# Attention with routing: one operand of routing's VectorE operations in PSUM, low parts of weights behind the row normalisation

## The chip, the cores and the metric

The kernel runs on one core of a Trainium2 chip. The metric is the device time of one execution in microseconds (us). Each engine has its own instruction stream: TensorE (PE in the rows) multiplies and transposes into PSUM, VectorE (DVE) and ScalarE (ACT) work on SBUF and PSUM, GpSimd (POOL) works on SBUF here, and SyncE (SP) issues DMAs. Engines wait for each other by semaphores.

## The reference

Four sequences of 768 positions with 8 heads of 64 go through attention with 4 sinks and a window of 128. The 3072 resulting rows of 512 then go through a mixture of experts in two levels: a group of four and an expert of four inside it, 16 experts with a hidden width of 1024.

```python
keep = is_sink | in_window                  # rel >= 0 and rel < 128
scores = np.where(keep, scale * q @ k.T, -1e9)
a = softmax(scores); x = (a @ v) as [N, D]  # N 3072, D 512
g_idx = argmax(x @ w_group); g_w = softmax(x @ w_group)[g_idx]
for g in range(G):
    xg = x[g_idx == g]
    e_idx = argmax(xg @ w_expert[g]); e_w = softmax(...)[e_idx]
    for e in range(Eg):
        out[tokens of g, e] = g_w * e_w * (relu(xg @ w1[g, e]) @ w2[g, e])
```

## The kernel before

All instructions of one engine run in the order in which the code is written (class `Pinned`; nearly all of them show its line 105, so the rows go by the names of tiles). Attention is a loop over 24 query tiles of 128 rows (line 1225), software-pipelined: iteration i scores tile i, and finishes tiles i-1 (`a`) and i-2 (`b`). Per iteration TensorE does, in order: scores of the first four heads into PSUM tile `ps0`, values of the second half of tile `b` (`po`), scores of the other four heads into `ps1`, transposes of the weights (`tp`), the transposed rows of `b`, the router logits (`ps<-wsd,xT`, in spare columns 208 to 247 of `ps0`), values of the first half of `a`, and sums over the sinks.

VectorE does `maxima` for both halves (COPY_PREDICATED and four reductions each, out of `ps0` and `ps1` into `sm` and `st`), the logits' normalisation `lw`, the rows' normalisation `xt` out of `po`, and two kinds of extra work. `po` has one buffer, so the values of the next iteration wait for `xt`. ScalarE does the exponentials and evacuations; GpSimd masks the window's weights (`halves`: `pw<-pw,tri`, 128x512, with both inputs in SBUF, twice per iteration).

The first kind of extra work on VectorE is routing. The 24 tiles are routed in four batches of six (`route_batch`, line 362). Three of them run while attention does: batch 0 alone, batch 1 with the pick of the first expert to load (`pick_id`, line 524), batch 2 with the second; the fourth runs after attention. A batch is a generator; `unit(k)` and `routing` take one step of it, one or two small VectorE instructions, at fixed places of an iteration: between the reductions of the second `maxima`, behind `lw` and behind `xt`. The batch's maxima, positions and keys (`m`, `rv`, `pos`, `ga` in tile `row`; `rs`, `cnt`, `key`, `idv`) all lie in SBUF.

The second kind is the splitting of expert weights, from iteration 18 on: ScalarE casts half a weight tile to `whi`, and VectorE subtracts, `wlo = rw - whi` (`wjob`, line 714; `low`, line 729), in halves of 128x512. The loop calls it as `late()` behind `lw` and ahead of `xt`. Behind attention comes the expert part, in which TensorE computes layers 1 and 2 out of `whi` and `wlo`.

Of the kernel before, what the change touches and what calls it, by code (L numbers as in the profile page):

```python
# [22 lines left out]
P = 128  # L23
# [10 lines left out]
NSK = 4  # L34
# [100 lines left out]
def moe_attention(tc, kqT, vN, vS, nsw, wgx, w1, w2, out):  # L135
    nc = Pinned(tc)
    v = nc.vector
    with ExitStack() as top, ExitStack() as att:
# [37 lines left out]
        nat = po2[:, :, 256:512]  # L176

# [184 lines left out]
        def route_batch(i0, nb, lt, wk, pt, tab, na, pick=None):  # L362
# [11 lines left out]
            lv = lt[:, 0:nb].rearrange("p n (k c) -> p n k c", c=4)  # L374
            nk = 1 + G

            def wide(t):
                return t[:, :, :, None].to_broadcast([P, nb, nk, 4])

            row = wk.tile([P, D], F32, name="row", bufs=1)  # L380
            m = row[:, 0:nb * nk].rearrange("p (n k) -> p n k", k=nk)
            pos, ga = (row[:, x:x + nb] for x in (MAXB * nk, MAXB * nk + MAXB))
            rv = row[:, MAXB * (nk + 2):MAXB * (nk + 2) + 4]
# [3 lines left out]
            d5 = rdt[:, 0:nb]  # L387
            d = d5[:, :, :, 0:4]
# [3 lines left out]
            v.scalar_tensor_tensor(o5.rearrange("p n k c -> p (n k) c"), d.rearrange("p n k c -> p (n k) c"), 0.0,  # L392
                                   rv[:, None, :].to_broadcast([P, nb * nk, 4]), ALU.is_ge, ALU.mult)
            yield
            v.tensor_reduce(m, o5, AX.X, ALU.max)
            yield
            v.tensor_tensor(o5, o5, wide(m), ALU.is_equal)
            yield
            og = o5[:, :, 0]
# [19 lines left out]
            if pick is not None:  # L419
                v.tensor_copy(cnt, pc)  # L420
            nc.scalar.activation(d, d, AF.Exp)
            yield
            if pick in (0, 1):
                yield from pick_id(wk, pick)
            rs = wk.tile([P, NE], F32, name="rs", bufs=1)
# [18 lines left out]
            s5, m = m, sm([G], "rm")  # L444
            v.tensor_reduce(s5, d5, AX.X, ALU.add)
            yield
            v.tensor_tensor(m, og, s5[:, :, 1:], ALU.mult)
            yield
            v.tensor_reduce(s5[:, :, 1], m, AX.X, ALU.add)
            yield  # L450
            ss = sm([2], "rss")
            v.reciprocal(ss, s5[:, :, 0:2])
# [54 lines left out]
        def select(wk, r, j0, j1):  # L507
            idv = wk.tile([P, NCOL], F32, name="idv", bufs=1)
# [15 lines left out]
        def pick_id(wk, r):  # L524
            key = wk.tile([P, NE], F32, name="key", bufs=1)
            tmp = wk.tile([P, NE], F32, name="ktmp", bufs=1)
            top = wk.tile([P, 1], F32, name="ktop", bufs=1)
            if r:
                v.tensor_tensor(tmp, oh01[:, 0], cnt, ALU.mult)
                v.tensor_reduce(cs0[:, 1:2], tmp, AX.X, ALU.add)  # L530
                yield
            v.scalar_tensor_tensor(key, cnt, float(NE), col[:, 0:NE], ALU.mult, ALU.subtract)
            if r:
                v.scalar_tensor_tensor(key, oh01[:, 0], -float(BIG), key, ALU.mult, ALU.add)
            yield
            v.tensor_reduce(top, key, AX.X, ALU.max)
            yield
            v.tensor_tensor(oh01[:, r], key, top.to_broadcast([P, NE]), ALU.is_equal)
            yield
            v.tensor_tensor(tmp, oh01[:, r], col[:, 0:NE], ALU.mult)  # L540
            v.tensor_reduce(top, tmp, AX.X, ALU.add)
            yield
            v.tensor_copy(eid01[:, r:r + 1], top)
            ready.add(f"id{r}")
            yield
            if r == 0:
                v.tensor_tensor(tmp, oh01[:, 0], cnt, ALU.mult)
# [203 lines left out]

        psb = [ps_s.tile([P, 4, 256], F32, name=f"ps{g}") for g in range(2)]
# [472 lines left out]
        for i in range(NI + 2):  # L1225
# [86 lines left out]
            if live:  # L1312
# [13 lines left out]
                put_gates(2)  # L1326
                routing(1, ("rd",))
# [311 lines left out]
```

## Time and profile before

| | us |
|---|---|
| median of 3 runs | 494.79 (494.03 to 496.2) |
| the profiled execution | 493.75 |
| span of its trace | 492.0 |
| busy in the span: TensorE | 462.5 (94%) |
| VectorE | 349.3 (71%) |
| ScalarE | 326.3 (66%) |
| GpSimd | 165.8 (34%) |

The profile shows the profiled execution, whose time exceeds the span by what lies around the first and last instruction. Attention fills about the first 150 us of it. A row of a timeline gives an instruction's start and its duration in us, the output and the inputs by the names of tiles, and in brackets how long the engine stood idle before it and which engine's work let it go on.

### The profile page before, as it was taken

Reading aid. Unit: us, or ns where it says so; the run is one execution under the profiler, and the core shown is the slowest. Engines: PE = TensorE matmul, PEld = TensorE weight load, DVE = VectorE, ACT = ScalarE, POOL = GpSimd, SP = SyncE. Lnnn points to the kernel's source line nnn. Section 1 sums busy time; section 2 is a strip of 40 time slices with the busy share of each in tenths; the row PEclk is TensorE's granted clock in tenths of the full one; section 3 lists DMA queues with packets and bytes.
Section 4 is the critical chain, followed back from the end, with each engine's and each line's share of the span. In section 5 each row is a group of like instructions: output and inputs, shape, how many; then the busy total and the mean of one; then the engine's idle time right before and its main releaser. Section 6 shows DMA issues by size and latency. Waiting matters only on the chain.

```text
span 492.0 us, 15509 instructions
## 1 busy us (share of the span) xinstructions
PE 462.5 (94%) x5865; PEld 393.9 (80%) x5865; DVE 349.3 (71%) x1141; ACT 326.3 (66%) x875; POOL 165.8 (34%) x269
## 2 busy tenths in 40 slices
PE   7999899877888999999999999999999999999994
PEld 6887778766767988989897878897879788877894
DVE  6766887896998789894157236763697888688870
ACT  4998889777875435583166266564878877677861
POOL 3463575555565303514122114020503070205021
PEclk9999999999999999999999999999999999999998
DMA  6575557566865539798015287967979997958200
GB/s 195 162 220 185 180 178 211 178 197 199 282 206 190 132 89 394 236 325 322 23 49 163 52 295 270 376 223 262 370 255 328 411 387 251 316 196 307 66 26 30
DMA packets 49557, 107.47 MB, mean 218 GB/s; under 512 B 8933, under 2 KB 9445, under 8 KB 49473
## 3 DMA queue, kind: packets, MB, share of 16 engines
q1 hardware_dynamic: 45008, 93.17, 56.1%
q0 software_dynamic: 4320, 12.94, 7.5%
q8 instruction: 48, 0.79, 0.7%
q14 instruction: 37, 0.30, 0.2%
q10 hardware_dynamic: 144, 0.28, 0.2%
HBM read 93.58 MB, written 12.93 MB: 216 GB/s over the span
## 4 chain that ended last, share of the span: by engine, by line
PE 66%; DVE 14%; issue 8%; ACT 7%; DMA 2%; POOL 1%; POOLq 0%; SPq 0%; DVEq 0%; ACTq 0%
PE po L105 29%; PE ph L105 27%; PE ps L105 5%; PE tp L105 5%; ACT pt L105 3%; DVE wlo L105 3%; DVE sm L105 2%; DVE xt L105 1%; ACT whi L105 1%; DVE un L105 1%; DMA kb<-in_kqT 1%; DMA qb<-in_kqT 1%; ACT pw L105 1%; POOL out L105 1%; DVE ps L105 1%
## 5 line engine op out<-in xcount | busy, mean ns | idle before, releaser
L105 DVE TENSOR_TENSOR wlo<-rw,whi 128x1024 fp32r<-128x1024 f32 (+1 forms) x116 | 134.5, 1184 | 30.4 <-ACT whi L105 30.0
L105 PE MATMUL ph<-un,whi 128*128 128x256 f32 (+9 forms) x576 | 128.7, 313 | 0.0
L105 PE MATMUL po<-whi,un 128*128 128x512 f32 (+6 forms) x384 | 126.3, 394 | 0.0
L105 ACT CAST whi<-rw 128x1024 fp32r<-128x1024 f32 (+1 forms) x116 | 114.8, 1018 | 5.9 <-PE po L105 3.2
L105 POOL DMA_INDIRECT out<-ot,sidx x33 | 42.2, 1279 | 220.4 <-ACT ot L105 163.8
L105 PE MATMUL ph<-un,wlo 128*128 128x160 f32 (+10 forms) x416 | 99.5, 264 | 0.7 <-DVE wlo L105 0.7
L105 PEld LDWEIGHTS ph<-un,whi 128*128 128x128 f32 x576 | 93.9, 189 | 2.4 <-issue 0.6
L105 PEld LDWEIGHTS po<-whi,un 128*128 128x128 f32 (+5 forms) x384 | 69.7, 183 | 19.5 <-issue 2.1
L105 ACT ACTIVATE pt<-sm,st 128x136 f32<-128x136 f32 x192 | 76.2, 404 | 7.1 <-DVE st L105 7.0
L105 PE MATMUL po<-wlo,un 128*128 128x512 f32 (+7 forms) x200 | 77.9, 389 | 0.0
L105 PEld LDWEIGHTS ph<-un,wlo 128*128 128x128 f32 x416 | 76.8, 189 | 1.3 <-DVE wlo L105 0.9
L105 POOL TENSOR_TENSOR pw<-pw,tri 128x512 f32<-128x512 f32 x40 | 51.2, 1279 | 22.7 <-ACT pw L105 22.2
L105 PE MATMUL po<-pw,vv 64*64 64x128 f32 (+1 forms) x1408 | 40.9, 250 | 12.7 <-DVE xt L105 9.4
L105 DVE CUSTOM_DVE_ANT_0 sm<-ps,msk 128x136 f32<-128x136 f32 x192 | 46.5, 295 | 6.9 <-ACT xT L105 1.3
L105 PEld LDWEIGHTS po<-pw,vv 64*64 64x64 f32 x1408 | 34.9, 133 | 19.5 <-POOL sp L105 8.3
L105 POOL DMA_INDIRECT xg<-xd,gidx x33 | 35.2, 1066 | 28.4 <-DMA rw<-in_w 16.5
L105 PE MATMUL ps<-kb,qb 64*64 64x204 f32 (+1 forms) x768 | 41.4, 330 | 2.2 <-DVE eid L105 0.9
L105 PEld LDWEIGHTS po<-wlo,un 128*128 128x128 f32 (+6 forms) x200 | 35.7, 178 | 7.9
L105 DVE TENSOR_TENSOR hc<-ph,hc 128x160 f32<-128x160 f32 (+6 forms) x64 | 21.5, 336 | 26.0 <-ACT hc L105 26.0
L105 ACT ACTIVATE un<-ph 128x256 fp32r<-128x256 f32 (+1 forms) x40 | 15.3, 384 | 36.7 <-PE ph L105 36.3
L105 ACT ACTIVATION_READ_ACCUMULATOR pt<-sm,st 128x1 f32 x192 | 37.1, 193 | 0.0
L105 ACT ACTIVATE ot<-po,cg 128x512 f32<-128x512 f32 (+7 forms) x25 | 17.0, 680 | 29.2 <-PE po L105 29.1
(201 smaller groups left out, 664.5 us busy)
## 6 DMA issues: line engine op xcount, KB each, us to landing
rw<-in_w SPq DMA_DIRECT2D x128, 512.0 KB, 5.5
kb<-in_kqT SPq DMA_DIRECT2D x23, 272.0 KB, 4.3
qb<-in_kqT SPq DMA_DIRECT2D x24, 256.0 KB, 4.1
vv<-in_vN SPq DMA_DIRECT2D x24, 256.0 KB, 3.5
xd<-xt SPq DMA_DIRECT2D x24, 256.0 KB, 2.4
xg<-xd,gidx POOLq DMA_INDIRECT x33, 5.9
out<-ot,sidx POOLq DMA_INDIRECT x33, 5.7
sv<-in_vS SPq DMA_DIRECT2D x4, 128.0 KB, 4.2
```

The lines of the kernel that those rows point to most:

```text
L105: r = f(*a, **k)
```

## The change

1. In the three early batches `m` and `rv` lie in spare columns of the PSUM tile `ps1` (`psb[1]` in the code, behind column `PART`); in batches 0 and 1 (`keep`) also `pos`, `ga`, `rs`, `cnt` (as `n_e`), `key`, `idv`, and the group part `og` of the one-hot, which a small instruction of its own computes. So one operand of most of these two-operand instructions lies in PSUM: 48 VectorE instructions touch these columns, none before. Patterns are reshaped to a form that fits four banks' spare columns. In batch 2 only `m` and `rv` move.
2. `pick_id` takes the expert's number out of a fused compare and product, casts it, and forms the one-hot `oh01` behind it.
3. `late()` stands behind `norm(b)` (`xt`) and the gates' DMAs; ahead of `norm(b)` stand always four `unit` calls, where they were two in iterations with a low part.

```diff
@@ -174,6 +174,8 @@
         tp2 = ps_p.tile([P, 2, 512], F32, name="tp")
         po2 = ps_a.tile([P, 2, 512], F32, name="po")
         nat = po2[:, :, 256:512]
+        psb = [ps_s.tile([P, 4, 256], F32, name=f"ps{g}") for g in range(2)]
+        PART = 3 * BW + NSK + MAXB
 
         def bank(pt):
             return pt.tile([P, 4, P], F32, name="tp")
@@ -371,32 +373,39 @@
                 if not early:
                     flush()
 
-            lv = lt[:, 0:nb].rearrange("p n (k c) -> p n k c", c=4)
-            nk = 1 + G
+            keep = early and pick in (None, 0)
+            nk, na2, ny = 1 + G, nb // 2, 2 * (1 + G)
+            lv = lt[:, 0:nb].rearrange("p n x -> p (n x)").rearrange("p (a y c) -> p a y c", a=na2, c=4)
 
             def wide(t):
-                return t[:, :, :, None].to_broadcast([P, nb, nk, 4])
+                return t[..., None].to_broadcast([P, na2, ny, 4])
 
             row = wk.tile([P, D], F32, name="row", bufs=1)
-            m = row[:, 0:nb * nk].rearrange("p (n k) -> p n k", k=nk)
-            pos, ga = (row[:, x:x + nb] for x in (MAXB * nk, MAXB * nk + MAXB))
-            rv = row[:, MAXB * (nk + 2):MAXB * (nk + 2) + 4]
+            m0 = row[:, 0:nb * nk].rearrange("p (a y) -> p a y", a=na2)
+            m = psb[1][:, 0:na2, PART:PART + ny] if early else m0
+            rv = psb[1][:, 3, PART:PART + 4] if early else row[:, D - 4:D]
+            pos, ga = (psb[1][:, x, PART + ny:PART + ny + nb] if keep else row[:, nb * (nk + x):nb * (nk + x + 1)] for x in (0, 1))
             v.tensor_copy(rv, rev)
             v.tensor_reduce(m, lv, AX.X, ALU.max)
             yield
-            d5 = rdt[:, 0:nb]
-            d = d5[:, :, :, 0:4]
+            d5 = rdt[:, 0:nb].rearrange("p n k x -> p (n k x)").rearrange("p (a y x) -> p a y x", a=na2, x=5)
+            d = d5[..., 0:4]
             v.tensor_tensor(d, lv, wide(m), ALU.subtract)
             yield
             o5 = sm([nk, 4], "req")
-            v.scalar_tensor_tensor(o5.rearrange("p n k c -> p (n k) c"), d.rearrange("p n k c -> p (n k) c"), 0.0,
+            o5n = o5.rearrange("p n k c -> p (n k) c")
+            o5a = o5n.rearrange("p (a y) c -> p a y c", a=na2)
+            v.scalar_tensor_tensor(o5n, rdt[:, 0:nb].rearrange("p n k x -> p (n k) x")[..., 0:4], 0.0,
                                    rv[:, None, :].to_broadcast([P, nb * nk, 4]), ALU.is_ge, ALU.mult)
             yield
-            v.tensor_reduce(m, o5, AX.X, ALU.max)
-            yield
-            v.tensor_tensor(o5, o5, wide(m), ALU.is_equal)
-            yield
-            og = o5[:, :, 0]
+            v.tensor_reduce(m, o5a, AX.X, ALU.max)
+            yield
+            og = psb[1][:, :, PART - nb:PART].rearrange("p c n -> p n c") if keep else o5[:, :, 0]
+            if keep:
+                o5b, mb = (t.rearrange("p a (b k) c -> p a b k c", k=nk) for t in (o5a, wide(m)))
+                v.tensor_tensor(og.rearrange("p (a b) c -> p a b c", a=na2), o5b[:, :, :, 0], mb[:, :, :, 0], ALU.is_equal)
+            v.tensor_tensor(o5a, o5a, wide(m), ALU.is_equal)
+            yield
             oh = wk.tile([P, nb, NE], BF16, name=f"oh{nb}", bufs=1)
             v.tensor_tensor(oh.rearrange("p n (g e) -> p n g e", g=G), o5[:, :, 1:],
                             og[:, :, :, None].to_broadcast([P, nb, G, EG]), ALU.mult)
@@ -417,12 +426,13 @@
             pe = sm([NE], "pe")
             v.tensor_tensor(pe, ppv, oh, ALU.mult)
             if pick is not None:
-                v.tensor_copy(cnt, pc)
+                n_e = psb[1][:, 3, PART:PART + NE] if keep else cnt
+                v.tensor_copy(n_e, pc)
             nc.scalar.activation(d, d, AF.Exp)
             yield
             if pick in (0, 1):
-                yield from pick_id(wk, pick)
-            rs = wk.tile([P, NE], F32, name="rs", bufs=1)
+                yield from pick_id(wk, pick, n_e, keep)
+            rs = psb[1][:, 1, PART:PART + NE] if keep else wk.tile([P, NE], F32, name="rs", bufs=1)
             v.tensor_reduce(rs, oh.rearrange("p n e -> p e n"), AX.X, ALU.add)
             yield
             v.tensor_tensor(runb, runb, rs, ALU.add)
...
-        def select(wk, r, j0, j1):
-            idv = wk.tile([P, NCOL], F32, name="idv", bufs=1)
+        def select(wk, r, j0, j1, keep=False):
+            idv = psb[1][:, 2, PART + 10:PART + 10 + EC] if keep else wk.tile([P, NCOL], F32, name="idv", bufs=1)
             idz = wk.tile([P, NCOL], F32, name="idz", bufs=1)
             sel = wk.tile([P, 3, NE], F32, name="sel", bufs=1)[:, 0:j1 - j0]
             v.tensor_tensor(sel, tab[:, :, j0:j1].rearrange("p e a -> p a e"),
@@ -521,37 +531,38 @@
                     later.append((r, j))
             yield
 
-        def pick_id(wk, r):
-            key = wk.tile([P, NE], F32, name="key", bufs=1)
+        def pick_id(wk, r, n_e, keep):
+            key = psb[1][:, 0, PART:PART + NE] if keep else wk.tile([P, NE], F32, name="key", bufs=1)
             tmp = wk.tile([P, NE], F32, name="ktmp", bufs=1)
             top = wk.tile([P, 1], F32, name="ktop", bufs=1)
+            eid = wk.tile([P, 1], F32, name="keid", bufs=1)
             if r:
-                v.tensor_tensor(tmp, oh01[:, 0], cnt, ALU.mult)
+                v.tensor_tensor(tmp, oh01[:, 0], n_e, ALU.mult)
                 v.tensor_reduce(cs0[:, 1:2], tmp, AX.X, ALU.add)
                 yield
-            v.scalar_tensor_tensor(key, cnt, float(NE), col[:, 0:NE], ALU.mult, ALU.subtract)
+            v.scalar_tensor_tensor(key, n_e, float(NE), col[:, 0:NE], ALU.mult, ALU.subtract)
             if r:
                 v.scalar_tensor_tensor(key, oh01[:, 0], -float(BIG), key, ALU.mult, ALU.add)
             yield
             v.tensor_reduce(top, key, AX.X, ALU.max)
             yield
-            v.tensor_tensor(oh01[:, r], key, top.to_broadcast([P, NE]), ALU.is_equal)
-            yield
-            v.tensor_tensor(tmp, oh01[:, r], col[:, 0:NE], ALU.mult)
-            v.tensor_reduce(top, tmp, AX.X, ALU.add)
-            yield
-            v.tensor_copy(eid01[:, r:r + 1], top)
+            v.scalar_tensor_tensor(tmp, key, top, col[:, 0:NE], ALU.is_equal, ALU.mult)
+            v.tensor_reduce(eid, tmp, AX.X, ALU.add)
+            yield
+            v.tensor_copy(eid01[:, r:r + 1], eid)
             ready.add(f"id{r}")
             yield
+            v.tensor_scalar(oh01[:, r], key, top, None, ALU.is_equal)
+            yield
             if r == 0:
-                v.tensor_tensor(tmp, oh01[:, 0], cnt, ALU.mult)
+                v.tensor_tensor(tmp, oh01[:, 0], n_e, ALU.mult)
                 v.tensor_reduce(cs0[:, 0:1], tmp, AX.X, ALU.add)
                 yield
 
         def route(i0, nb, lt, pick):
             yield from route_batch(i0, nb, lt, rk, None, tab, MAXA, pick)
             if pick == 0:
-                yield from select(rk, 0, 0, EC)
+                yield from select(rk, 0, 0, EC, True)
             elif pick == 1:
                 yield from select(rk, 0, EC, NTR[0])
                 ready.add("late")
@@ -748,8 +759,6 @@
 
             half.append(more)
             return lambda: low(0, z)
-
-        psb = [ps_s.tile([P, 4, 256], F32, name=f"ps{g}") for g in range(2)]
 
         def lg(i):
             o = 3 * BW + NSK
@@ -1315,15 +1324,15 @@
                 flush()
                 exps(i, 1)
                 trans(i, 0)
-                if late:
-                    late()
-                for k in range(2 if late else 4):
+                for k in range(4):
                     unit(k)
                 if old:
                     norm(b)
                 if later and not gates:
                     gather(*later.pop(0))
                 put_gates(2)
+                if late:
+                    late()
                 routing(1, ("rd",))
                 routing(1, ("hv",))
                 for k in range(2):
```

The instructions of TensorE, ScalarE, GpSimd and SyncE keep their order. VectorE's order and some waits change. The first place is VectorE at the first pick (iterations 16 and 17; `ps_99` is the PSUM tile of the second score group, `ps_98` or `ps_210` the first). Before:

```order
L105 TENSOR_TENSOR ktmp<-oh_200,col 128x16
L105 TENSOR_REDUCE ktop<-ktmp 128x1
L105 TENSOR_REDUCE rc<-sacc_189 128x16
L105 RECIPROCAL rc<-rc 128x16
L105 TENSOR_TENSOR lw<-ps_210,rc 128x160
L105 CAST eid_204<-ktop 128x1
L105 TENSOR_TENSOR ktmp<-oh_200,cnt 128x16
L105 TENSOR_REDUCE cs_201<-ktmp 128x1
L105 TENSOR_REDUCE rs<-oh_2164 128x16
L105 TENSOR_TENSOR runb<-runb,rs 128x16
L105 TENSOR_TENSOR xt<-po,rc 128x2x4x64
```

At the same place in the changed kernel:

```order
L105 CAST eid_206<-keid 128x1
L105 TENSOR_REDUCE rc<-sacc_191 128x16
L105 RECIPROCAL rc<-rc 128x16
L105 TENSOR_TENSOR lw<-ps_98,rc 128x160
L105 TENSOR_SCALAR oh_202<-ps_99,ktop 128x16
L105 TENSOR_TENSOR ktmp<-oh_202,ps_99 128x16
L105 TENSOR_REDUCE cs_203<-ktmp 128x1
L105 TENSOR_REDUCE ps_99<-oh_2165 128x16
L105 TENSOR_TENSOR runb<-runb,ps_99 128x16
L105 TENSOR_TENSOR xt<-po,rc 128x2x4x64
```

The product with `col` has moved up between the reductions and reads the key from PSUM; the cast stands ahead of `lw`; `runb` and the count's product have one operand in PSUM.

The second place is VectorE at the first low parts (iteration 18; two halves there). Before:

```order
L105 TENSOR_REDUCE rc<-sacc_190 128x16
L105 RECIPROCAL rc<-rc 128x16
L105 TENSOR_TENSOR lw<-ps_210,rc 128x160
L105 TENSOR_TENSOR wlo<-rw,whi 128x512 x2
L105 TENSOR_TENSOR xt<-po,rc 128x2x4x64
L105 TENSOR_TENSOR bf<-colm,row 128x384
L105 COPY_PREDICATED ps_210<-selu,ps_210 128x4x64
```

And in the changed kernel:

```order
L105 TENSOR_REDUCE rc<-sacc_192 128x16
L105 RECIPROCAL rc<-rc 128x16
L105 TENSOR_TENSOR lw<-ps_98,rc 128x160
L105 TENSOR_TENSOR xt<-po,rc 128x2x4x64
L105 TENSOR_TENSOR wlo<-rw,whi 128x512 x2
L105 TENSOR_TENSOR bf<-colm,ps_99 128x384
L105 COPY_PREDICATED ps_98<-selu,ps_98 128x4x64
```

`xt` no longer stands behind the two low parts; `bf` still does, and it now reads `ps_99`. That gives TensorE a new wait at the start of iteration 19. Its rows there in the changed kernel, with the semaphores that each waits for:

```order
L105 MATMUL ps_98<-kb,qb 64x204 [waits DMAHW7_49,DMAHW0_49,DVE_49]
L105 MATMUL ps_98<-kb,qb 64x204 x7
L105 MATMUL po<-pw,vv 64x128 [waits DVE_49,Pool_49]
L105 MATMUL po<-pw,vv 64x128 x3
L105 MATMUL po<-pw,vv 64x64 x4
L105 MATMUL po<-pw,vv 64x128 x4
L105 MATMUL po<-pw,vv 64x64 x4
L105 MATMUL ps_99<-kb,qb 64x204 [waits DVE_49]
L105 MATMUL ps_99<-kb,qb 64x204 x7
```

In the kernel before the eight matmuls of the second group (`ps_211` there) stand without a wait; ten iterations (9, 10, 12, 13, 15, 16, 17, 19, 20 and 21) have the new one, on the last VectorE instruction that touches the spare columns.

The third place is VectorE at the start of batch 2 (iteration 22). Before:

```order
L105 COPY row<-rev 128x4
L105 TENSOR_REDUCE row<-lt 128x30
L105 TENSOR_TENSOR lw<-ps_210,rc 128x160
L105 TENSOR_TENSOR wlo<-rw,whi 128x512
L105 TENSOR_TENSOR rdt<-lt,row 128x30x4
L105 SCALAR_TENSOR_TENSOR req<-rdt,row 128x120
L105 TENSOR_TENSOR xt<-po,rc 128x2x4x64
L105 TENSOR_REDUCE row<-req 128x30
L105 TENSOR_TENSOR req<-req,row 128x120
L105 COPY_PREDICATED ps_210<-selu,ps_210 128x4x64
```

And in the changed kernel:

```order
L105 COPY ps_99<-rev 128x4
L105 TENSOR_REDUCE ps_99<-lt 128x3x10
L105 TENSOR_TENSOR lw<-ps_98,rc 128x160
L105 TENSOR_TENSOR rdt<-lt,ps_99 128x30x4
L105 SCALAR_TENSOR_TENSOR req<-rdt,ps_99 128x120
L105 TENSOR_REDUCE ps_99<-req 128x3x10
L105 TENSOR_TENSOR req<-req,ps_99 128x120
L105 TENSOR_TENSOR xt<-po,rc 128x2x4x64
L105 TENSOR_TENSOR wlo<-rw,whi 128x512
L105 TENSOR_TENSOR oh_3190<-req 128x96
L105 COPY_PREDICATED ps_98<-selu,ps_98 128x4x64
```

Here the low part and two steps of routing have changed sides of `xt`, and the one-hot `oh` stands ahead of the next COPY_PREDICATED instead of between the reductions behind it, with both inputs still in SBUF.

## Rows read from the trace of the kernel before

**Rows 1.** Windows: stretch, us, busy of PE PEld DVE ACT POOL, clock, DMA share, GB/s.
```profile
46.00:152.00 106.00, 89.78 (x2368) 75.39 (x2368) 89.62 (x425) 86.67 (x348) 60.49 (x106) 1.00 0.65 204
152.00:470.00 318.00, 315.46 (x2374) 268.49 (x2364) 222.68 (x508) 195.62 (x360) 78.47 (x74) 1.00 0.69 241
```

**Rows 2.** Waits of TensorE, 46 to 152 us: total us, times, longest us.
```profile
PE po L105 <- DVE xt L105: 9.4, 8, 2.6
PE ps L105 <- DVE st L105: 2.1, 4, 0.9
```

**Rows 3.** Timeline of VectorE: start, duration, operation, [idle before, releaser].
```profile
54.84 0.99 DVE L105 TENSOR_TENSOR req<-req,row 128x120 f32<-128x120 f32 x1
64.51 0.89 DVE L105 TENSOR_TENSOR ge<-row,edge 128x48 f32<-128x48 f32 x1
99.97 1.01 DVE L105 TENSOR_TENSOR ktmp<-oh,col 128x16 f32<-128x16 f32 x1
102.63 1.14 DVE L105 TENSOR_TENSOR runb<-runb,rs 128x16 bf16<-128x16 bf16 x1
107.75 0.97 DVE L105 SCALAR_TENSOR_TENSOR row<-ga,row 128x6 f32<-128x6 f32 x1
130.68 1.28 DVE L105 SCALAR_TENSOR_TENSOR sidx<-idv,idz 128x2 uint32<-128x2 f32 x1
137.76 1.28 DVE L105 TENSOR_TENSOR req<-req,row 128x120 f32<-128x120 f32 x1
167.58 0.28 DVE L105 TENSOR_TENSOR req<-req,row 128x120 f32<-128x120 f32 x1
```

**Rows 4.** Timeline of GpSimd: one masking of `pw`.
```profile
102.48 1.27 POOL L105 TENSOR_TENSOR pw<-pw,tri 128x512 f32<-128x512 f32 x1 [0.24 <-ACT pw L105]
```

**Rows 5.** Timeline of TensorE: groups with idle time before them.
```profile
66.29 0.92 PE L105 MATMUL ps<-kb,qb 64*64 64x204 f32 x16 [0.62 <-DVE lw L105]
92.99 0.66 PE L105 MATMUL ps<-wsd,xT 128*64 128x40 f32 x16 [0.45 <-DVE st L105]
102.08 0.92 PE L105 MATMUL ps<-kb,qb 64*64 64x204 f32 x16 [0.91 <-DVE eid L105]
104.52 0.90 PE L105 MATMUL po<-pw,vv 64*64 64x128 f32 x32 [1.52 <-POOL lw L105]
110.58 0.90 PE L105 MATMUL po<-pw,vv 64*64 64x128 f32 x32 [0.83 <-DVE xt L105]
118.40 0.90 PE L105 MATMUL po<-pw,vv 64*64 64x128 f32 x32 [2.58 <-DVE xt L105]
124.16 0.56 PE L105 MATMUL po<-pw,vv 64*64 64x128 f32 x16 [0.62 <-DVE xt L105]
133.36 0.67 PE L105 MATMUL ps<-wsd,xT 128*64 128x40 f32 x16 [0.93 <-DVE st L105]
137.69 0.90 PE L105 MATMUL po<-pw,vv 64*64 64x128 f32 x32 [0.88 <-DVE xt L105]
140.43 0.67 PE L105 MATMUL ps<-wsd,xT 128*64 128x40 f32 x16 [0.45 <-DVE st L105]
142.64 0.22 PE L105 MATMUL tp<-oh,trib 128*128 128x96 bf16 x1 [0.71 <-DVE oh L105]
```

**Rows 6.** Timeline of VectorE: a low part of the weights.
```profile
116.97 0.69 DVE L105 TENSOR_TENSOR wlo<-rw,whi 128x512 fp32r<-128x512 f32 x1 [1.38 <-ACT whi L105]
```

**Rows 7.** VectorE with and without PSUM operands: timeline, last the page's group (total, mean ns).
```profile
48.99 0.43 DVE L105 COPY_PREDICATED ps<-selu,ps 128x256 f32<-128x256 int32 x1 [0.37 <-PE ps L105]
49.57 0.30 DVE L105 CUSTOM_DVE_ANT_0 sm<-ps,msk 128x136 f32<-128x136 f32 x1
60.84 0.25 DVE L105 TENSOR_TENSOR pe<-tp,oh 128x96 f32<-128x96 f32 x1
167.89 0.26 DVE L105 TENSOR_TENSOR oh<-req 128x96 bf16<-128x96 f32 x1
L105 DVE CUSTOM_DVE_ANT_0 sm<-ps,msk 128x136 f32<-128x136 f32 x192 | 46.5, 295 | 6.9 <-ACT xT L105 1.3
```

More of the change, by code (lines that the diff above doesn't have):

```diff
@@ L443, in route_batch @@
             yield
-            s5, m = m, sm([G], "rm")
-            v.tensor_reduce(s5, d5, AX.X, ALU.add)
+            s5, rm = m0.rearrange("p a (b k) -> p a b k", k=nk), sm([G], "rm")
+            v.tensor_reduce(m0, d5, AX.X, ALU.add)
             yield
-            v.tensor_tensor(m, og, s5[:, :, 1:], ALU.mult)
+            v.tensor_tensor(rm.rearrange("p (a b) g -> p a b g", a=na2), og.rearrange("p (a b) g -> p a b g", a=na2), s5[..., 1:], ALU.mult)
             yield
-            v.tensor_reduce(s5[:, :, 1], m, AX.X, ALU.add)
+            v.tensor_reduce(s5[..., 1], rm.rearrange("p (a b) g -> p a b g", a=na2), AX.X, ALU.add)
             yield
             ss = sm([2], "rss")
-            v.reciprocal(ss, s5[:, :, 0:2])
+            v.reciprocal(ss.rearrange("p (a b) k -> p a b k", a=na2), s5[..., 0:2])
             cw = wk.tile([P, MAXB, GW], F32, name="cw", bufs=2)[:, 0:nb]
```

## The prediction

> **What bounds the kernel now.** I read the windows first. From 152 us to 470 us TensorE is busy 315.46 of 318.00 us at full clock: whatever attention saves ahead of that, the end gets one for one, as long as the weights keep up [rows 1]. From 46 to 152 us TensorE is busy 89.78 of 106.00 us, so 16.2 us are idle; VectorE, with 89.62, is as loaded [rows 1]. The view of waits says who is late: 9.4 us, in 8 waits, are values (`po`) that wait for the row normalisation `xt`, and 2.1 us, in 4, are logits that wait for `st`, the maxima [rows 2]. Both are VectorE's. So the end is set, in this stretch, by VectorE's order and by every VectorE instruction ahead of `xt`, of the maxima and of the logits' normalisation `lw`.
>
> The timeline then shows which instructions are long for their size. `req<-req,row` over 128x120 takes 0.28 us at 167.58, but 0.99 at 54.84 and 1.28 at 137.76; `ktmp` and `runb`, over 16 columns, take 1.01 and 1.14, `ge` 0.89, `row<-ga,row` over six columns 0.97, and `sidx` over two 1.28 [rows 3]. `runb` ends at 102.63 + 1.14 = 103.77; GpSimd's `pw`, which began at 102.48, ends at 102.48 + 1.27 = 103.75 [rows 3, 4]. A tiny instruction with two SBUF operands that meets `pw` stretches to the end of it.
>
> **The change part by part.** For TensorE, each stall that such an instruction causes is worth the idle time in front of its matmuls, and no more. Without contention I give an instruction of 16 columns or fewer 0.2 us, an estimate by the 0.28 of `req`, which has 120 [rows 3].
>
> *Compares of the first steps.* `req` now reads `m` from PSUM. In batch 0 it loses 0.99 - 0.28 = 0.7 us at 54.84 [rows 3], but I take nothing there. In batch 1 the logits at 92.99 waited 0.45 us for `st` behind it [rows 5]; I take 0.45.
>
> *`ge`.* It loses 0.89 - 0.2 = 0.7 us; the `lw` behind it held the scores at 66.29 for 0.62 us [rows 3, 5]. What is late next is unknown; 0.5.
>
> *The first pick.* `ktmp` stood ahead of `lw` and the cast `eid`, `runb` ahead of `xt`: excess 1.01 - 0.2 and 1.14 - 0.2, together 1.75 [rows 3]. TensorE stood idle 0.91 us at 102.08 and 1.52 at 104.52, 2.43 in all [rows 5]. The second wait is put down to GpSimd's `lw`, which itself follows VectorE's. I take 1.5, under the excess, since GpSimd's `pw` and the values stay in their order.
>
> *`ga`.* It loses 0.97 - 0.2 = 0.77; the values at 110.58 waited 0.83 for the `xt` behind it [rows 3, 5]. 0.7.
>
> *Low parts behind `xt`, iterations 18 and 19.* The values at 118.40 waited 2.58 us for `xt`, those at 124.16 0.62 [rows 5]. In the first place `xt` stood behind two `wlo`; the second of them had itself waited 1.38 us for ScalarE's `whi` and then took 0.69 [rows 6]. Both leave `xt`'s path, 2.07 us. But `wlo` now stands ahead of `bf`, the COPY_PREDICATED of the maxima, and by `bf` ahead of the scores' new wait, so ScalarE's lateness comes back there. The move hands back at most 2.58 + 0.62 = 3.2, at least nothing; I take 1.3, the 0.69 of each `wlo` nearly whole and none of the wait for ScalarE.
>
> *`sidx`.* It loses about 1.1 us of its 1.28, and the logits at 133.36 waited 0.93 for the maxima behind it [rows 3, 5]. But a `wlo` of 0.69 [rows 6] now stands there instead, and the scores wait for `sidx`: 0.93 - 0.69 = 0.24, so 0.25.
>
> *Batch 2.* `req` (1.28) shrinks by 1.0 [rows 3]; the idle times around it were 0.88, 0.45 and 0.71, together 2.04 [rows 5]. `xt` gives up one `wlo` ahead of it and gets two more steps of routing, about 0.28 each, so that exchange is worth only 0.1. `oh` keeps two SBUF inputs and follows `wlo`; if it meets `pw`, 1.1 of the gain is lost, leaving 0.9. I take 1.4, between 0.9 and the 2.04 at most.
>
> Sum of gains: 0.45 + 0.5 + 1.5 + 0.7 + 1.3 + 0.25 + 1.4 = 6.1 us.
>
> **What it adds.** The two instructions for `og` are 0.4 us on an engine that has slack in their iterations, behind the logits' wait: 0 to 0.4, taken as 0. Twenty of the 48 instructions write to PSUM what a next one reads. The row that shows such a pair is COPY_PREDICATED: it ends at 48.99 + 0.43 = 49.42, its reader starts at 49.57, 0.15 later, where an SBUF pair takes 0.03 (167.58 + 0.28, then 167.89) [rows 3, 7]. Per pair that is 0.12; mostly it lies between maxima or in slack, so I take three pairs on the path, about 0.3. An instruction itself is not longer with a PSUM operand: `pe<-tp,oh` 0.25, `oh<-req` 0.26, of the same 96 columns [rows 7].
>
> Ten second groups of scores wait for a VectorE instruction behind `xt`. Ahead of them stand 0.90 us of values, which also start on `xt` [rows 5], so an instruction that ends within 0.9 us of `xt` costs nothing; queued behind a wait are the transposes and logits, and VectorE's second maxima wait for the scores. One 0.69 `wlo` and `bf` can overrun that; I take 0.1 in all.
>
> Net gain 6.1 - 0.4 = 5.7 us: 493.75 - 5.7 = 488.05 for a run like the profiled one. That one lies 1.04 under the median, so the forecast is 494.79 - 5.7 = 489.1.
>
> **The rivals.**
>
> *PSUM is dearer than the rows show.* All twenty pairs on the path cost 20 x 0.12 = 2.4, and the three new waits of iterations 19 to 21 overrun by 0.69 + 0.69 - 0.90 = 0.48 each, 1.4, if a `bf` is as long as a `wlo` [rows 5, 6]. The gain falls to 6.1 - 2.4 - 1.4 = 2.3: 492.5. For it: the gap at 49.42; against it: most pairs stand where TensorE has work. [...]
>
> *The change doesn't do what it says.* If a PSUM operand doesn't free an instruction from `pw`, only the move of `wlo` works: 494.79 - 1.3 = 493.5. For it: no row shows routing's small instructions with a PSUM operand beside a `pw`. Against it: `sm<-ps,msk` has one operand in PSUM and one in SBUF, and its 192 executions have a mean of 295 ns, no more than the single one's 0.30, though GpSimd masks `pw` in every iteration [rows 7].
>
> *Slower: `wlo` meets `pw`.* Five single `wlo` follow iteration 18, with two SBUF operands, now directly behind `xt`; the `req` of 1.28 at 137.76 stood one reduction behind `xt`, so a `pw` began close to `xt` there [rows 3, 4]. If each waits a whole `pw`, 5 x 1.27 = 6.4 us fall on COPY_PREDICATED and the new wait, while 0.45 + 0.5 + 1.5 + 0.7 = 3.15 of the gain stay: 494.79 + 3.2 = 498. It decides from three of five on. Against it: `wlo` starts at once behind `xt`, mostly ahead of `pw`. [...]
>
> **How the numbers follow.** Forecast 0.68, dearer PSUM 0.17, no effect of PSUM 0.07, slower 0.08. A measurement of this kernel can tell 0.5%, 2.5 us, from no change: faster means below 492.3. The forecast's own range is 486 to 491.5: the unknowns are 1.3 (0 to 3.2), 1.5 (0 to 2.43) and 1.4 (0.9 to 2.04). Of the dearer case, around 492.5, just under half (0.08) counts as faster, and all of the forecast's does: 0.76. Within: its other part, 0.09, and the third case, 0.16. Slower: 0.08. The range, which takes in the second and third case, is 485.8 to 493.5.
>
> **What would show it.** Right: no instruction on routing's PSUM columns above 0.4 us beside a `pw`; `xt` no longer releasing 9.4 us of waits from 46 to 152 us, but under 6; TensorE's idle time there near 10.5; the expert part as long as before. Wrong: `runb`, `ktmp` or `ga` still near 1 us; waits `ps <- DVE bf` or `runb` of over 0.3 us each; `wlo` near 1.3 us; or the expert part waiting for weights, so that the saving is lost behind 152 us.

## The result and the profile after

The changed kernel takes 487.86 us (median of 4 runs, 487.55 to 488.47) against 494.76 for the kernel before in the same comparison: a ratio of 0.9859, with an interval of 0.9834 to 0.9883, so 6.9 us or 1.4% faster. The forecast was 489.1 with a range of 485.8 to 493.5. The profiled execution took 487.55 us with a span of 485.7. One execution of the kernel before in the comparisons below was slow, 711.31 us at a granted clock of 0.574, and no median or ratio here contains it.

The windows view of the changed kernel, as in [rows 1]. Attention ends some 6 us sooner, so the stretches end 6 us sooner too:

```profile
46.00:146.00 100.00, 89.72 (x2357) 75.48 (x2359) 81.76 (x427) 85.84 (x347) 59.46 (x105) 1.00 0.68 217
146.00:464.00 318.00, 315.68 (x2375) 269.00 (x2376) 222.79 (x508) 196.10 (x362) 77.48 (x74) 1.00 0.69 241
```

TensorE does the same work, 89.72 us of it, in 100 us instead of 106; its idle time fell from 16.2 to 10.3. In the expert part nothing moved: 315.68 of 318 against 315.46 of 318. VectorE's load in the stretch fell from 89.62 to 81.76, 7.9 us, though it executes two instructions more.

The waits of TensorE from 46 to 146 us in the changed kernel (total us, times, longest), as in [rows 2]:

```profile
PE po L105 <- POOL sp L105: 2.3, 2, 1.7
PE po L105 <- DVE ps L105: 2.2, 2, 1.2
PE ps L105 <- DVE bf L105: 2.1, 2, 1.6
PE ps L105 <- DVE st L105: 1.2, 2, 0.9
PE po L105 <- DVE xt L105: 0.8, 1, 0.8
PE ps L105 <- DVE sidx L105: 0.8, 1, 0.8
PE po L105 <- DVE row L105: 0.5, 1, 0.5
```

`xt` released 9.4 us of waits before and 0.8 now, but part of that is a change of names. Two waits of 2.2 with the name `ps` belong to it too, since the values follow `xt` and the routing steps ahead of it. So do the 2.3 of `sp`, a copy on GpSimd: `xt` ended 0.09 and 0.10 us ahead of it in the two places, and the longer one, 1.67 at 145.92, was this wait before:

```profile
151.68 0.90 PE L105 MATMUL po<-pw,vv 64*64 64x128 f32 x32 [1.86 <-DVE xt L105]
```

With them `xt` holds 5.3 us of waits of `po` where it held 9.4. New are 2.9 us of scores that wait for `bf` and `sidx`.

VectorE's instructions that answer to [rows 3], in its timeline (start, duration):

```profile
52.97 0.28 DVE L105 TENSOR_REDUCE ps<-lt 128x30 f32<-128x120 f32 x1
53.29 0.28 DVE L105 TENSOR_TENSOR rdt<-lt,ps 128x120 f32<-128x120 f32 x1
...
54.92 0.28 DVE L105 TENSOR_TENSOR req<-req,ps 128x120 f32<-128x120 f32 x1
...
64.38 0.20 DVE L105 TENSOR_TENSOR ge<-ps,edge 128x48 f32<-128x48 f32 x1
...
104.92 0.17 DVE L105 SCALAR_TENSOR_TENSOR ps<-ga,ps 128x6 f32<-128x6 f32 x1
...
126.71 0.16 DVE L105 SCALAR_TENSOR_TENSOR sidx<-ps,idz 128x2 uint32<-128x2 f32 x1
...
132.77 1.33 DVE L105 TENSOR_TENSOR oh<-req 128x96 bf16<-128x96 f32 x1
```

And GpSimd's masking at the same times, with [rows 4] as its counterpart:

```profile
54.36 1.28 POOL L105 TENSOR_TENSOR pw<-pw,tri 128x512 f32<-128x512 f32 x1 [0.28 <-ACT pw L105]
...
104.45 1.28 POOL L105 TENSOR_TENSOR pw<-pw,tri 128x512 f32<-128x512 f32 x1 [1.17 <-ACT pw L105]
...
126.69 1.28 POOL L105 TENSOR_TENSOR pw<-pw,tri 128x512 f32<-128x512 f32 x1 [1.48 <-ACT pw L105]
...
132.58 1.41 POOL L105 TENSOR_TENSOR pw<-pw,tri 128x512 f32<-128x512 f32 x1 [0.28 <-ACT pw L105]
```

The reader is to lay the one over the other. `req` at 54.92, the `ga` step at 104.92 and `sidx` at 126.71 lie whole inside a `pw` and take 0.28, 0.17 and 0.16 us, where they took 0.99, 0.97 and 1.28. `oh` at 132.77, whose two inputs stayed in SBUF, meets a `pw` and takes 1.33. The first two rows show what a result in PSUM costs the next instruction: the reduction ends at 53.25 and its reader starts at 53.29.

TensorE's idle times that replace those of [rows 5]:

```profile
114.54 0.92 PE L105 MATMUL ps<-kb,qb 64*64 64x204 f32 x16 [1.61 <-DVE bf L105]
119.81 0.92 PE L105 MATMUL ps<-kb,qb 64*64 64x204 f32 x16 [0.49 <-DVE bf L105]
126.92 0.92 PE L105 MATMUL ps<-kb,qb 64*64 64x204 f32 x16 [0.76 <-DVE sidx L105]
...
135.49 0.67 PE L105 MATMUL ps<-wsd,xT 128*64 128x40 f32 x16 [0.85 <-DVE st L105]
...
145.92 0.90 PE L105 MATMUL po<-pw,vv 64*64 64x128 f32 x32 [1.67 <-POOL sp L105]
```

Since TensorE's order is the same in all kernels here, the start of the 22 groups of logits gives a measure by place: the difference of a group's start in two kernels, from one group to a later one, is what the stretch between them gained (-) or lost (+). The table has these differences against the kernel before, in us, worked out from the timelines. Its columns run from group 4 to 7, 7 to 8, 8 to 11, 13 to 14, 14 to 16, 16 to 17, 17 to 19, 19 to 20, and from 20 to the first matmul of the expert part (`ph<-ident,xg`); "to first experts" is the whole way from group 4. The experiments below are in it.

| kernel | up to group 7 | batch 0 compare | `ge` | batch 1 compare | pick | `ga` | low parts | `sidx` | batch 2 | to first experts |
|---|---|---|---|---|---|---|---|---|---|---|
| changed | -0.59 | -0.45 | -0.51 | -0.45 | -1.50 | -0.69 | -1.03 | -0.20 | -0.88 | -6.30 |
| after_again | -0.26 | -0.45 | -0.62 | -0.44 | -1.51 | -0.68 | -1.06 | -0.21 | -0.89 | -6.12 |
| e1_move | -0.54 | -0.01 | -0.11 | -0.01 | 0.00 | -0.02 | -1.33 | +0.65 | -0.35 | -1.72 |
| e2_psum | -0.54 | -0.46 | -0.63 | -0.43 | -1.50 | -0.69 | +1.22 | -0.91 | -1.53 | -5.47 |
| e3_sbuf | -0.85 | +0.29 | +0.23 | +0.30 | -1.42 | +0.10 | -1.33 | +0.65 | -0.30 | -2.33 |
| e4_m_only | -0.54 | -0.37 | +0.35 | -0.36 | -1.43 | +0.09 | -0.30 | +0.65 | -0.43 | -2.34 |
| e5_late_last | -0.82 | -0.46 | -0.62 | -0.45 | -1.52 | -0.68 | -1.88 | +0.58 | -1.67 | -7.52 |
| e6_pick | -0.81 | -0.02 | -0.12 | -0.01 | -1.43 | +0.08 | 0.00 | -0.02 | -0.08 | -2.41 |
| e7_oldpick | -0.55 | -0.46 | -0.61 | -0.45 | -0.95 | -0.33 | -1.04 | -0.20 | -0.83 | -5.42 |
| e8_batch2 | -0.53 | -0.46 | -0.64 | -0.45 | -1.51 | -0.68 | -1.03 | -0.20 | -2.01 | -7.51 |
| e9_both | -0.82 | -0.47 | -0.62 | -0.44 | -1.50 | -0.69 | -1.87 | +0.58 | -1.59 | -7.42 |
| e10_order | -0.82 | 0.00 | -0.09 | -0.01 | -1.43 | +0.09 | -1.33 | +0.65 | -0.45 | -3.39 |
| e11_two | -1.09 | -0.51 | -0.64 | -0.50 | -1.29 | -0.77 | -1.87 | +0.57 | -1.76 | -7.86 |

The first column is no part of the change: `e6_pick`, which differs from the kernel before only from iteration 14 on, has it too. It is some 0.3 to 0.8 us of delay that the one profiled execution of before had around iteration 5. Without it the changed kernel gained 5.7 us by place. Counted from the span's start the two kernels are even there (group 7 starts at 50.59 and 50.55): of the 6.3 us between the spans, 5.7 lie between group 7 and the first experts and some 0.5 behind.

Two rows hold a stretch of lower clock besides. In the profiled executions of `e2_psum` and `e4_m_only`, and in no other here, TensorE's granted clock fell during attention: over the whole execution its mean was 0.986 and 0.990, in all the others 0.996 to 0.998. So their entries for the low parts are not the work of their order alone (see `e2_psum`).

The granted clock also helps to explain why medians and places differ. Of the kernel before's 54 executions in the experiments' comparisons 39 had a mean granted clock below 0.995, of the changed kernel's ten, four here and six in `after_again`, one; the others lie at 0.995 to 0.998. In the comparison that holds `after_again`, the kernel before took 491.89 and 493.12 us in its two executions at 0.997, with a median of 494.97; the changed kernel took 487.06 to 488.10 in its five at 0.996 or more. At like clock that is some 5.1 us, by the medians 7.5. So part of the medians' gain is clock that the kernel before was not granted. Why it was granted less, no run here shows.

### The profile page after: what moved, and what is told of

Its sections match the earlier page's. It is cut to its first block, busy times and chain, and to the rows that moved or that the text cites. A ratio compares the mean times of both kernels' runs of the same rounds, so it can differ in the third digit from the quotient of the medians.

```text
span 485.7 us, 15514 instructions
## 1 busy us (share of the span) xinstructions
PE 462.8 (95%) x5865; PEld 394.7 (81%) x5865; DVE 341.5 (70%) x1143; ACT 325.9 (67%) x875; POOL 163.8 (34%) x269
## 4 chain that ended last, share of the span: by engine, by line
PE 65%; DVE 13%; issue 8%; ACT 6%; DMA 4%; POOL 2%; SPq 1%; POOLq 0%; DVEq 0%; ACTq 0%
PE po L105 29%; PE ph L105 28%; PE tp L105 4%; PE ps L105 4%; DVE wlo L105 3%; ACT pt L105 2%; DVE sm L105 2%; DVE xt L105 2%; ACT whi L105 1%; DMA rw<-in_w 1%; DVE un L105 1%; DMA vv<-in_vN 1%; DVE ps L105 1%; DMA ni<-in_nsw 1%; SPq L105 1%
```

## The experiments

Each was compared with the kernel before on the same chip; its median there was 494.29 us for e1 to e4, 493.92 for e5 to e8, and 494.97 for e9 to e11 and after_again.

**e1_move: the move of the low parts alone.** The last of the three changes, on the kernel before:

```diff
-                if late:
-                    late()
-                for k in range(2 if late else 4):
+                for k in range(4):
                     unit(k)
...
                 put_gates(2)
+                if late:
+                    late()
                 routing(1, ("rd",))
```

> Of the change only the move of the low parts behind the row normalisation, with four steps of routing ahead of it; every operand of routing stays in SBUF. Theory (the gain comes from operands in PSUM, which no longer stretch beside GpSimd's masking): 1.0 to 1.3 us of gain at iterations 18 and 19 alone, so 493.5 to 493.8, and req, runb, ktmp and ga are as long as before (about 1 us). Rival (the order is what counts): most of the 6.9 us, so 490 or less.

492.22 us, ratio 0.9961 (0.9939 to 0.9984): faster by 2.1, with an interval of 0.8 to 3.0 that holds the theory's 1.0 to 1.3 and not the rival's 4.3. By place it gains 1.33 at the low parts and 0.35 at batch 2 and loses 0.65 at `sidx`, 1.0 in all. TensorE's timeline at the two places:

```profile
119.37 0.67 PE L105 MATMUL ps<-wsd,xT 128*64 128x40 f32 x16 [1.19 <-DVE st L105]
...
132.45 0.66 PE L105 MATMUL ps<-wsd,xT 128*64 128x40 f32 x16 [1.76 <-DVE st L105]
```

The wait for `xt` is gone, and the logits wait for the maxima behind the low parts instead, 1.19 and 1.76 us; the second of these was 0.93 in [rows 5]. In batches 0 and 1 `req`, `runb`, `ktmp` and `ga` stayed as long as they were.

**e2_psum: the change without the move.** That piece of the diff undone, everything else kept.

> The changed kernel with the low parts back ahead of the row normalisation and two steps of routing beside them: the PSUM operands and the reordered pick alone. Theory: it keeps all but the 1.0 us of the move, so about 489. Rival (order): 492 or more.

488.60 us, ratio 0.9874 (0.9842 to 0.9906): 5.7 faster, as the theory has it. Its timelines at the low parts, VectorE and then TensorE:

```profile
113.47 0.69 DVE L105 TENSOR_TENSOR wlo<-rw,whi 128x512 fp32r<-128x512 f32 x1 [1.36 <-ACT whi L105]
```
```profile
114.91 1.56 PE L105 MATMUL po<-pw,vv 64*64 64x128 f32 x32 [2.58 <-DVE xt L105]
116.22 1.55 PE L105 MATMUL ps<-kb,qb 64*64 64x204 f32 x16
```

TensorE waits the same 2.58 us as in [rows 5]. By place it loses 1.22 us here, but that is clock: the granted clock, 1.00 here in the kernel before, had a mean of 0.54 in the 2 us around the end of the wait and of 0.60 in the next 2. The windows view of e2, columns as in [rows 1]:

```profile
114.00:116.00 2.00, 1.09 (x24) 1.12 (x28) 1.97 (x7) 0.00 (x0) 1.25 (x3) 0.54 0.19 68
116.00:118.00 2.00, 2.00 (x39) 1.34 (x34) 0.72 (x7) 1.37 (x5) 0.00 (x0) 0.60 0.63 117
```

Values and scores took 1.56 and 1.55 us; in the kernel before, whose clock from 118 to 122 us stayed at 1.00 behind the same wait, they took 0.90 each. In the profiled execution of `e4_m_only` the same happened behind waits of 1.19 and 1.77 us: scores took 1.64 us at 120.16 and values 1.52 at 132.22. In e10, behind waits of 1.18 and 1.76, the scores at 119.67 took 0.92 and no such stretch followed; nor did one in e1, behind 1.19 and 1.76, with a mean clock of 0.997 like e10's. Why the clock fell in some executions and not in others, no run here shows.

So beside the PSUM operands the move is not priced. The intervals of e2 and of the changed kernel overlap, and e2 gains 1.36 more at `sidx` and batch 2 (-0.91 and -1.53 against -0.20 and -0.88), where its `oh` met no `pw` and took 0.25 us. That the move is worth 1.0 us is shown in SBUF alone, by e1 and again by e10 against e6.

**e3_sbuf: the same order and patterns, in SBUF.**

```diff
+        sbp = const([P, 4, MAXB + 24], F32, "sbp")
-            m = psb[1][:, 0:na2, PART:PART + ny] if early else m0
+            m = sbp[:, 0:na2, PART:PART + ny] if early else m0
...
```

> The changed kernel in order and patterns, but what it puts into spare PSUM columns lies in an SBUF tile of its own instead, so the scores' new waits go too. Theory: the small instructions stretch to about 1 us again beside the masking, and the time comes back to 493 to 494, that of the move alone. Rival 1 (order and the fused pick bring the gain): 489.5 or less. [...]

492.83 us, ratio 0.9975 (0.9955 to 0.9996): rival 1 falls. VectorE's timeline shows the stretching come back, and on an instruction that the kernel before does not have, the group part of the one-hot:

```profile
54.64 0.89 DVE L105 TENSOR_TENSOR sbp<-req,sbp 128x24 f32<-128x24 f32 x1
...
64.60 0.88 DVE L105 TENSOR_TENSOR ge<-sbp,edge 128x48 f32<-128x48 f32 x1
...
90.31 1.08 DVE L105 TENSOR_TENSOR sbp<-req,sbp 128x24 f32<-128x24 f32 x1
```

At the three places of `req` and `ge` it is slower than before by 0.2 to 0.3 each. But at the pick it keeps 1.42 of 1.50 us. There the theory was wrong: `ktmp` and `runb` were short without PSUM, as in e6 (0.28 and 0.17 us). Since the two kernels differ only in where the operands lie and in the waits that follow from it, this is what shows that the place of the operands matters: without the first column, 1.5 us by place against the changed kernel's 5.7.

**e4_m_only: only `m` and `rv` in PSUM.** `keep = False`.

> The changed kernel with only m and rv in PSUM, in all three batches; pos, ga, og, rs, cnt, key and idv are back in SBUF. Theory: what belongs to ge (0.6), the first pick (1.5), ga (0.7) and sidx (0.2) is lost, 3.0 us, so about 491; ktmp, runb, ge and ga near 1 us again. Rival (each PSUM operand costs, and the compares of m bring nearly all): 488 or less.

490.30 us, ratio 0.9920 (0.9893 to 0.9947). The sum came close to the 491 expected, its parts not: the compares kept 0.37 and 0.36 of their 0.45, `ge`, `ga` and `sidx` lost theirs as expected, and some more, but the pick again kept 1.43. Its -0.30 at the low parts holds the lower clock named above. From VectorE's timeline:

```profile
54.38 0.27 DVE L105 TENSOR_TENSOR req<-req,ps 128x120 f32<-128x120 f32 x1
...
63.77 0.89 DVE L105 TENSOR_TENSOR ge<-row,edge 128x48 f32<-128x48 f32 x1
```

**e6_pick: the reordered pick alone.** The new `pick_id` in the kernel before, all in SBUF:

```diff
-            v.tensor_tensor(oh01[:, r], key, top.to_broadcast([P, NE]), ALU.is_equal)
-            yield
-            v.tensor_tensor(tmp, oh01[:, r], col[:, 0:NE], ALU.mult)
-            v.tensor_reduce(top, tmp, AX.X, ALU.add)
+            v.scalar_tensor_tensor(tmp, key, top, col[:, 0:NE], ALU.is_equal, ALU.mult)
+            v.tensor_reduce(eid, tmp, AX.X, ALU.add)
...
```

> The kernel before with only the reordered pick (fused compare and product, cast, one-hot behind it), all in SBUF. Theory (the pick's gain is one of order: the product with col leaves the place where it met the masking): about 1.4 us, 492.9, and no ktmp or runb near 1 us in iterations 16 and 17. Rival (the gain needs the PSUM operands): 494 or more, and ktmp or runb near 1 us.

493.05 us, ratio 0.9981 (0.9956 to 1.0005). The runs as a whole don't tell it from no change. At like clock they nearly do: of its five executions at 0.996 or more four took 490.67 to 490.98 and one 492.76, the kernel before's four 492.68 to 492.75. And the trace has 1.43 us at the pick and, but for the first column, nothing above 0.12 elsewhere. VectorE and GpSimd there:

```profile
98.47 0.28 DVE L105 SCALAR_TENSOR_TENSOR ktmp<-key,ktop,col 128x16 f32<-128x16 f32 x1
...
101.11 0.17 DVE L105 TENSOR_TENSOR runb<-runb,rs 128x16 bf16<-128x16 bf16 x1
```
```profile
98.67 1.28 POOL L105 TENSOR_TENSOR pw<-pw,tri 128x512 f32<-128x512 f32 x1
...
101.51 1.27 POOL L105 TENSOR_TENSOR pw<-pw,tri 128x512 f32<-128x512 f32 x1 [0.28 <-ACT pw L105]
```

Both now start just ahead of a `pw`. The theory holds.

**e7_oldpick: the old order of the pick, in PSUM.** The same piece undone in the changed kernel.

> The changed kernel with the old order of the pick, its key, counts and sums in PSUM. Theory (a PSUM operand frees an instruction wherever it stands): only the product with col, whose two operands stay in SBUF, is long again, 0.8 us, so 488.7. Rival 1 (the order brought it all): 1.5 us lost, 489.4. Rival 2 (neither order matters once PSUM is used): 487.9.

487.91 us, ratio 0.9872 (0.9847 to 0.9896); 0.0013 above the changed kernel's ratio, 0.6 us, which the intervals don't separate. By place 0.55 of the pick's and 0.36 of `ga`'s gain are lost. VectorE and TensorE:

```profile
97.91 0.98 DVE L105 TENSOR_TENSOR ktmp<-oh,col 128x16 f32<-128x16 f32 x1
```
```profile
99.99 0.92 PE L105 MATMUL ps<-kb,qb 64*64 64x204 f32 x16 [0.90 <-DVE eid L105]
```

Of the pick's instructions only the product with two SBUF operands is long, as the theory said. So order alone gave 1.43 and PSUM alone 0.95 at a place where both give 1.50: either cures the same wait.

**e10_order: pick and move, no PSUM.** e1 and e6 together. **after_again: the changed kernel as it is**, in the same rounds.

> The kernel before with the reordered pick and the moved low parts, and no operand in PSUM: all that is order in the change. If the parts add up (2.1 and 1.0 to 1.4 us), 3.1 to 3.5 us under before, about 491; then the PSUM operands are worth the other 3.5 us. Rival (order and PSUM overlap, so that order alone has nearly all): 489 or less.

> The changed kernel as it is, for a comparison on the same chip and in the same rounds: 1.4% under before, 487 to 488.

490.50 us, ratio 0.9914 (0.9884 to 0.9943), and 487.45 us, ratio 0.9851 (0.9816 to 0.9887). The rival falls: order gives 4.5 us here and the PSUM operands 3.05 more. By place order gives 2.6 without the first column, about what e1 and e6 add up to; at a clock of 0.996 or more the medians are 492.5 (two executions of before), 490.1 (four of e10) and 487.4 (five of the changed kernel), so 2.4 and 2.7 us. By place the operands are worth most at `sidx`, 0.85. VectorE and TensorE of e10:

```profile
128.10 1.28 DVE L105 SCALAR_TENSOR_TENSOR sidx<-idv,idz 128x2 uint32<-128x2 f32 x1
```
```profile
130.77 0.67 PE L105 MATMUL ps<-wsd,xT 128*64 128x40 f32 x16 [1.76 <-DVE st L105]
```

With the low part moved ahead of a `sidx` that still meets a `pw`, both stand ahead of the maxima, and 0.65 us are lost where the changed kernel gains 0.20.

**e5_late_last: low parts at the end of the iteration.** `late()` behind the routing steps that follow `xt`, so that `bf` and `sidx` no longer stand behind it:

```diff
-                if late:
-                    late()
                 routing(1, ("rd",))
                 routing(1, ("hv",))
                 for k in range(2):
                     unit(k)
+                if late:
+                    late()
```

> The changed kernel with the low parts one place later still: behind bf, tab and the index work, so that the scores of the second group no longer wait for an instruction that stands behind a low part. Theory (that wait is on the path): the idle times 1.61, 0.49 and 0.76 of the scores go, logits then wait for the maxima instead, and 1 to 1.5 us are gained, about 486.6. Rival (the maxima stand behind the low parts in either order and set the end): no difference, 487.9.

486.02 us, ratio 0.9831 (0.9808 to 0.9854). The new waits for `bf` and `sidx` are gone, and 0.85 us more are gained at the low parts, but 0.78 are lost at `sidx`. VectorE and GpSimd there:

```profile
124.96 1.72 DVE L105 TENSOR_TENSOR wlo<-rw,whi 128x512 fp32r<-128x512 f32 x1
...
131.94 0.25 DVE L105 TENSOR_TENSOR oh<-req 128x96 bf16<-128x96 f32 x1
```
```profile
124.85 1.28 POOL L105 TENSOR_TENSOR pw<-pw,tri 128x512 f32<-128x512 f32 x1 [0.54 <-ACT pw L105]
```

This is the prediction's slower case at one of its places: `wlo` met a `pw` and took 1.72 instead of 0.69. In turn `oh`, now ahead of `wlo`, ran before the next `pw` and took 0.25. The expected gain came, 1.4 us by the ratios, but the two places that the theory named bring only 0.07 of it, 0.85 less 0.78; 0.79 come from batch 2, where `oh` was short.

**e8_batch2: the one-hot's group part, counts, key and sums of batch 2 in PSUM too.**

```diff
-            og = psb[1][:, :, PART - nb:PART].rearrange("p c n -> p n c") if keep else o5[:, :, 0]
+            og = psb[1][:, :, PART - nb:PART].rearrange("p c n -> p n c") if early else o5[:, :, 0]
...
```

> The changed kernel in which batch 2 too has og, the counts, the key and the sums in PSUM. Theory (ports): its oh falls from 1.33 to about 0.26 and the product of the second pick from 0.82 to 0.2, the logits behind them no longer wait 0.85 and 0.40, and 1.2 us are gained, 486.7. Rival (the next wait, GpSimd's sums or the new waits of the scores, takes over): within 0.4 us of 487.9.

486.43 us, ratio 0.9834 (0.9811 to 0.9857): the expected 1.2 us, and by place 1.13 more than the changed kernel at batch 2. That ports are the cause, no run shows; the traces show that `oh` and `ktmp`, with one operand in PSUM, took 0.24 and 0.23 us where the changed kernel's took 1.33 and 0.82. VectorE:

```profile
132.48 0.24 DVE L105 TENSOR_TENSOR oh<-req,ps 128x96 bf16<-128x96 f32 x1
...
142.11 0.23 DVE L105 SCALAR_TENSOR_TENSOR ktmp<-ps,ktop,col 128x16 f32<-128x16 f32 x1
```

**e9_both: e5 and e8 together, and e11_two: that with two routing steps ahead of `xt` and four behind it.**

> The changed kernel with both: low parts last in the iteration, and batch 2's og, counts, key and sums in PSUM. If the two gains (1.4 and 1.2 us by their ratios) add up, 2.6 us under the changed kernel, about 484.9; if both take away the same idle time of iterations 22 and 23, about 1.8, 485.7. This is the candidate that is to beat both kernels.

> As the candidate with both, and only two steps of routing ahead of the row normalisation, four behind it. Theory (the two waits of 1.05 and 1.15 us for the normalisation in iterations 8 and 14 come from steps ahead of it): they halve, about 1 us is gained, 484. Rival (steps behind it delay the maxima and the scores' new waits by as much): no gain, or slower.

486.72 us, ratio 0.9835 (0.9800 to 0.9870), and 486.64 us, ratio 0.9839 (0.9804 to 0.9875). Their medians lie 0.7 and 0.8 us below the changed kernel's in the same rounds: e9's six runs lie from 486.14 to 487.09, those of after_again from 487.06 to 488.10. Neither has what was expected. In e9 batch 2 gains no more than in e5 (1.59 and 1.67), since e5's order had made `oh` short already: the two took away the same wait, more so than the rival had it. e11 took the two waits at the batches' starts down, but the second matmul of layer 1 then waited (total, times, longest; 136 to 165 us):

```profile
PE ph L105 <- DVE un L105: 1.1, 1, 1.1
```

In e5 and e9 that wait is 0.3 and 0.5. That lies behind the table's last column. Which of e5, e8, e9 and e11 is fastest the runs don't tell.

## Why the prediction was right

**What bounds the kernel** held. Attention's gain came through to the end one for one, and the expert part stayed at 2.3 idle us in 318 (2.5 before).

**Contention with `pw`** held where it was put on PSUM: with order alone (e10) the compares, `ge` and `ga` gain nothing, with PSUM (e2) 0.46, 0.63, 0.43 and 0.69. Predicted were 0 for batch 0's compare, 0.5, 0.45 and 0.7. The zero was wrong by 0.45: the logits behind it had waited for the maxima too, if less than those of batch 1:

```profile
57.66 0.67 PE L105 MATMUL ps<-wsd,xT 128*64 128x40 f32 x16 [0.29 <-DVE st L105]
```

That the place of the operand is the cause is shown by e3. The prediction's signs of being right held: of the 48 instructions on routing's columns none that met a `pw` took more than 0.3 us in the changed kernel, `xt` holds 5.3 us of waits (under 6), and TensorE's idle time is 10.3 us (near 10.5).

**The first pick** has the right size, 1.5 for 1.5, by a cause that the prediction missed. It gave the gain to the shortening of `ktmp` and `runb` by PSUM; e6 has 1.43 of it from the order alone, in SBUF, because both instructions then start ahead of a `pw` and take 0.28 and 0.17 us.

**The low parts** were put at 1.3, with 0.1 for the scores' new waits. Measured are 1.03. The 3.2 us of idle time did go, and 2.1 came back as waits for `bf`. These look like a price of the PSUM columns, but e1, without the columns, gains only 1.33: there the logits wait instead, behind the same low parts and the same late `whi`. So the columns cost 0.3, not 2.1. Still, waits for `bf` of over 0.3 us were a sign of being wrong in the prediction's own list, and they came, 1.61 and 0.49: the scores' new wait was under-sized, at 0.1 for 0.3. What the move adds beside the PSUM operands is not shown (e2).

**`sidx`** gave 0.20 for 0.25. **Batch 2** gave 0.88 for 1.4: `oh` met the `pw`, the case that the prediction priced at 0.9, and e8 got the missing 1.1.

**What it adds** was put at 0.3 for slower pairs through PSUM. The pair in the profile after has a gap of 0.04 us, like one in SBUF; of 14 neighbouring pairs through routing's columns 12 have a gap of 0.03 to 0.04, and two overlap. The 0.15 of [rows 7] does not carry over: in either kernel 34 of the 40 COPY_PREDICATED of attention have such a gap behind them, 0.14 or 0.15, the other six 0.03 or 0.04. The rival of dearer PSUM falls with it.

**The sum** came out by luck in part. By terms it is 5.7, the forecast's 5.7, but the terms that were too high (0.27 at the low parts, 0.05 at `sidx`, 0.52 at batch 2) and those that were too low or charged for nothing (0.45 at batch 0's compare, 0.3 for the pairs, 0.1 for the scores' wait, whose price is in the low parts' 1.03) cancel. The time, 487.86, lies 1.2 under the forecast of 489.1. The forecast had added 1.04 us, by which the kernel before's median lay above its profiled execution; the changed kernel's median lies only 0.31 above. The later comparisons show why such an offset needn't carry over: most of the kernel before's executions ran at a lower clock, and nine of the changed kernel's ten did not. In the first comparison the clock of before is on record only for the profiled execution, 0.997.

## What to carry to other kernels

Lay the timelines of VectorE and GpSimd over each other before costing small VectorE instructions: here the seven of 0.89 to 1.28 us in [rows 3] ended 0.01 to 0.14 us behind the end of a `pw`. With one of its two operands moved to PSUM `req` took 0.28 us instead of 0.99; moved out of the `pw`'s way, `runb` took 0.17 instead of 1.14 (e6). Where both applied to one wait, the gains didn't add: 1.43 us and 0.95 alone, 1.50 together. A moved instruction carried its own contention to the new place: `wlo` took 1.72 us in e5. Where the granted clock differs between executions, compare those of like clock before a gain is put down to the change.

## What the runs showed of the hardware

`wlo` of e5, with two SBUF operands, started inside a `pw`: it began at 124.96, 0.11 us into a `pw` that ended at 126.13, and ended at 126.68, 0.55 later, after 1.72 us where a `wlo` elsewhere took 0.69. The other order is in e1, GpSimd first and then VectorE:

```profile
133.21 1.28 POOL L105 TENSOR_TENSOR pw<-pw,tri 128x512 f32<-128x512 f32 x1 [1.21 <-DMA rw<-in_w]
136.72 1.68 POOL L105 TENSOR_TENSOR pw<-pw,tri 128x512 f32<-128x512 f32 x1 [0.27 <-ACT pw L105]
```
```profile
133.76 0.75 DVE L105 COPY row<-rev 128x4 f32<-128x4 f32 x1
...
136.58 0.68 DVE L105 TENSOR_TENSOR wlo<-rw,whi 128x512 fp32r<-128x512 f32 x1
```

A `wlo` that started 0.14 us ahead of a `pw` kept its 0.68, and the `pw` took 1.68. And a copy of four columns from SBUF to SBUF, with one operand, also stretched to the end of a `pw`, 134.51 against 134.49: it took 0.75 us, where the same copy with its result in PSUM took 0.17 in the changed kernel, at 129.69 inside a `pw` that lasted from 129.07 to 130.37.
